# Loading batch 0's queries in halves, v of a pair in one load, and a lag for the Sinkhorn totals

## The chip, the cores and the metric

The kernel runs on one core of one Trainium2 chip. The metric is the device time of one execution in microseconds (us). The profiles list the program's instructions by engine: TensorE (PE, with its weight loads as PEld), VectorE (DVE), ScalarE (ACT), GpSimd (POOL, which here issues nearly all loads) and SyncE (SP). All runs compared here are fast; one run of the kernel before, at 988.76 us and a mean granted clock of 0.656, was slow and is left out.

## The reference, cut to what matters

Attention over 4 batches of 8 heads, 768 positions of 64 numbers, with a local band and 24 block summaries as keys. Its output is x (3072 x 512) for a mixture of 8 experts, all of which take every token, weighted by a matrix P that eight Sinkhorn rounds normalise by rows and columns. The attention lines are written shorter here than in the reference.

```python
k_sum = k.reshape(B, H, nb, 32, D).max(axis=3)
v_sum = v.reshape(B, H, nb, 32, D).mean(axis=3)
scores_l = scale * q @ k.T            # kept where |i - j| < 16
scores_s = scale * q @ k_sum.T + log(32)
out = softmax([scores_l, scores_s]) @ [v, v_sum]
...
P = np.exp(logits)
for _ in range(8):
    P /= P.sum(1, keepdims=True) + 1e-09
    P /= P.sum(0, keepdims=True) + 1e-09
    P *= N / E
for e in range(E):
    out += P[:, e:e+1] * (np.maximum(x @ w1[e], 0) @ w2[e])
```

## The kernel before

Heads are worked on in pairs, four pairs per batch. A small list scheduler (`Plan`) decides in Python, from estimated durations, in what order each engine gets its instructions. In the finished program that order is fixed, and in the runs below an engine whose next instruction is not ready waits for it: TensorE stands 3.0 us before two products whose data come late (no_lag), and only 1.7 us when the same products stand later in its order (the changed kernel).

The front, which the change is about, in cuts:

```python
def load_qk(i, z):                       # k or q of a pair, batch 0: one load
    ...
    nc.gpsimd.dma_start(
        out=t[:].rearrange("p j g d -> p j (g d)"),
        in_=src[b, h0:h0 + 2].rearrange("j (p g) d -> p j (g d)", g=G))

def load_v(i):                           # v of a pair: one load per head
    b, h0 = i // PB, (i % PB) * 2
    for j in range(2):
        nc.gpsimd.dma_start(out=v_x[i % NQ][:, :, j, 0:D],
                            in_=v[b, h0 + j].rearrange("(g p) d -> p g d", p=128))
...
nc.vector.memset(zeros, 0.0)
keep_busy(14)                            # 14 products of zeros
...
load_pair(0)                             # k, q, v
U["ident"] = last[0] = add("POOL", 0.35, ident_constant, [last[0]])
load_pair(1, "kq")
U["band"] = last[0] = add("POOL", 0.7, band_constants, [last[0]])
load_pair(2, "kq")
load_pair(1, "v")
load_pair(3, "kq")
load_pair(2, "v")
load_pair(3, "v")
for i in range(2):
    load(("w1", i), lambda i=i: load_w1_0(i), 0.85, 2.5)
load("w2", lambda: load_w2(0), 0.85, 5.0)
...
for i in range(PB):
    pair_start(i, i)                     # transposes of k and q, block maxima and sums
    pair_half(i, 0, i)                   # first halves of the queries
add("DVE", 1.6, late_constants, [U["mk", 0, 0]], 5.5)   # memsets that batch 1 needs
expert0(0, [U["x", i, 0] for i in range(PB)])           # expert 0 on the first halves
for i in range(PB):
    pair_half(i, 1, 10 + i)
...
plan.idle = (0.43, lambda: keep_busy(2), U["rl", 0, 0]) # fillers where PE would idle
```

And one round of Sinkhorn, in the "bridge" between attention and the seven remaining experts:

```python
for eng, us, fn, o, w in (("DVE", 0.5, rows, (), ()), ("POOL", 0.7, by_rows, (), ()),
                          ("DVE", 0.35, columns, (), ()), ("PE", 0.12, totals, [buf], ()),
                          ("DVE", 0.2, inverse, (), [buf]), ("POOL", 0.7, by_columns, (), ())):
    step = add(eng, us, fn, [step], -50.0, opens=o, uses=w)
```

The softmax here doesn't subtract the row's maximum and nothing guards it: scores larger than these inputs give would overflow.

## Time and profile before

The time was 687.12 us, the median of three runs. I cut the profiled execution into five parts.

| part | from, to | length in us |
|---|---|---|
| start | span start, first transpose of k | 5.71 |
| front | ... first product of expert 0's hidden layer | 21.12 |
| bulk | ... logits of the last batch | 101.65 |
| bridge | ... first product of the experts' second layer | 46.83 |
| tail | ... end | 509.79 |

### The profile page before, as it was taken

How to read it: one execution, taken by the hardware profiler on the slowest of the kernel's cores; microseconds unless marked ns; L12 is line 12 of the kernel's file. 1: busy time of each engine (PE TensorE's matmuls, PEld its weight loads, DVE VectorE, ACT ScalarE, POOL GpSimd, SP SyncE). 2: the span in 40 equal slices, each digit the busy share in tenths (PEclk: the TensorE clock that was granted, in tenths of full speed). 3: DMA queues.
4: the chain of work that ended last, by engine and by line, in shares of the span. 5: the costliest groups of instructions: out<-in, count | busy, mean ns of one | idle time of the engine just before them, and what ended most of it. 6: DMA issues, size and time to landing. Idle time of an engine off the chain costs nothing.

```text
span 685.1 us, 13613 instructions
## 1 busy us (share of the span) xinstructions
PE 673.9 (98%) x5195; PEld 439.0 (64%) x5195; DVE 590.4 (86%) x1440; ACT 404.7 (59%) x781; POOL 141.5 (21%) x189
## 2 busy tenths in 40 slices
PE   8999999999999999999999999999999999999996
PEld 4666656555666666666666666666666666666665
DVE  6779888797699998999889988998899888998886
ACT  5677677555677765555555555555555555555551
POOL 8599840121203120100101010201010101100000
PEclk9999999999999999999999999999999999999999
DMA  9999990000324023220513050403131051301224
GB/s 134 182 131 127 117 139 10 2 1 0 54 25 44 6 27 52 26 22 1 78 16 32 1 77 1 47 1 57 22 31 17 5 74 16 33 1 47 84 87 154
DMA packets 112786, 33.90 MB, mean 49 GB/s; under 512 B 98129, under 2 KB 109905, under 8 KB 112721
## 3 DMA queue, kind: packets, MB, share of 16 engines
q0 software_dynamic: 103840, 26.22, 40.3%
q1 hardware_dynamic: 8352, 6.80, 3.3%
q8 instruction: 41, 0.67, 0.4%
q14 instruction: 25, 0.20, 0.1%
q10 hardware_dynamic: 528, 0.02, 0.0%
HBM read 52.45 MB, written 6.29 MB: 86 GB/s over the span
## 4 chain that ended last, share of the span: by engine, by line
PE 85%; DVE 10%; issue 2%; DMA 1%; POOL 1%; ACT 0%; DVEq 0%; ACTq 0%
PE xy L837 32%; PE pg L831 14%; PE pb L831 9%; PE pa L831 9%; PE yps L204 6%; PE hps L199 6%; DVE hf L781 3%; DVE out_acc L974 2%; PE sg L301 1%; PE tkq L282 1%; DVE hf L892 1%; PE vs L309 1%; DVE hf L778 1%; DMA vx<-in_v_dram 1%; PE av L446 1%
## 5 line engine op out<-in xcount | busy, mean ns | idle before, releaser
L837 PEld LDWEIGHTS <-hf 128*128 128x128 f16 x2352 | 229.8, 98 | 99.2 <-issue 5.2
L837 PE MATMUL xy<-w,hf 128*128 128x256 f16 x1312 | 183.4, 273 | 0.0
L837 PE MATMUL xy<-ws,hf 128*128 128x256 f16 x984 | 147.6, 272 | 1.4
L190 ACT ACTIVATE hf<-pg 128x512 f16<-128x512 f32 x84 | 50.2, 597 | 158.2 <-PE pg L831 158.2
L974 DVE SCALAR_TENSOR_TENSOR out_acc<-xy,P_sb,out_acc 128x512 f32<-128x512 f32 x164 | 115.1, 744 | 1.7 <-PE xy L837 1.7
L778 DVE TENSOR_TENSOR hf<-hf 128x512 f16<-128x512 f16 x252 | 99.5, 422 | 3.2
L831 PE MATMUL pa<-xT,w 128*128 128x512 f16 x336 | 99.9, 379 | 0.0
L781 DVE TENSOR_TENSOR hf<-pb,c 128x512 f16<-128x512 f32 x84 | 58.0, 690 | 36.3 <-ACT xy L956 31.4
L831 PEld LDWEIGHTS <-w 128*128 128x128 f16 x672 | 65.6, 98 | 28.2 <-issue 0.5
L175 POOL DMA_DIRECT2D w<-in_moe_w_dram x56 | 41.8, 758 | 186.8 <-PE pg L831 181.3
L831 PEld LDWEIGHTS <-ws 128*128 128x128 f16 x504 | 49.3, 98 | 42.3 <-issue 0.2
L190 ACT ACTIVATE hf<-pa 128x512 f16<-128x512 f32 x84 | 50.2, 597 | 19.3 <-PE pa L831 19.3
L781 DVE TENSOR_TENSOR hf<-pg,c 128x512 f16<-128x512 f32 x84 | 57.2, 681 | 0.3
L850 ACT COPY pg<-pa 128x512 f32<-128x512 f32 x84 | 47.9, 570 | 5.0 <-PE pa L831 0.3
L831 PE MATMUL pg<-xTs,w 128*128 128x512 f16 x168 | 50.0, 379 | 0.1
L831 PE MATMUL pb<-xT,ws 128*128 128x512 f16 x168 | 50.0, 379 | 0.0
L831 PE MATMUL pb<-xTs,ws 128*128 128x512 f16 x168 | 50.0, 379 | 0.0
L831 PE MATMUL pg<-xTs,ws 128*128 128x512 f16 x168 | 50.0, 379 | 0.0
L858 ACT COPY c<-pb 128x512 f32<-128x512 f32 x84 | 49.7, 592 | 0.4 <-ACT pg L850 0.4
L831 PE MATMUL pg<-xT,w 128*128 128x512 f16 x168 | 49.8, 377 | 0.0
L199 PE MATMUL hps<-xT,w 128*128 128x384 f16 x256 | 49.3, 326 | 0.0
L865 ACT COPY c<-pg 128x512 f32<-128x512 f32 x84 | 48.7, 579 | 0.3 <-PE pg L831 0.3
(135 smaller groups left out, 859.6 us busy)
## 6 DMA issues: line engine op xcount, KB each, us to landing
w<-in_moe_w_dram POOLq DMA_DIRECT2D x8, 1024.0 KB, 9.2
w<-in_moe_w_dram POOLq DMA_DIRECT2D x56, 128.0 KB, 3.5
out_dram<-out_acc SPq DMA_DIRECT2D x22, 256.0 KB, 2.1
vx<-in_v_dram POOLq DMA_DIRECT2D x32, 96.0 KB, 4.9
kst<-in_k_dram POOLq DMA_DIRECT2D x24, 96.0 KB, 4.5
qst<-in_q_dram POOLq DMA_DIRECT2D x24, 96.0 KB, 4.3
w<-in_moe_w_dram POOLq DMA_DIRECT2D x2, 512.0 KB, 7.8
kst<-in_k_dram POOLq DMA_DIRECT2D x4, 192.0 KB, 4.9
```

The lines of the kernel that those rows point to most:

```text
L175: nc.gpsimd.dma_start(out=t[:, :, h, :], in_=moe_w1[e].rearrange("(dk p) f -> p dk f", p=128)[:, :, f:f + 128])
L190: nc.scalar.activation(out=out, in_=in_, func=AF.Relu, bias=0.0, scale=1.0)
L199: nc.tensor.matmul(hp[:, 0:n], lhsT=w1s[e][:, dk, 128 * f:128 * (f + 1)], rhs=xT[:, dk, t0:t0 + n], start=(dk == 0), stop=(dk == KD - 1))
L204: nc.tensor.matmul(yp[:], lhsT=h[:, f, c * 128:(c + 1) * 128], rhs=w2s[e][:, f, :], start=(f == 0), stop=(f == KF - 1))
L778: nc.vector.tensor_tensor(out=out, in0=in0, in1=in1, op=ALU.subtract)
L781: nc.vector.tensor_tensor(out=out, in0=in0, in1=in1, op=ALU.add)
L831: nc.tensor.matmul(bank[:], lhsT=w[:, dk, :], rhs=x[:, dk, :], start=start and dk == 0, stop=dk == KH - 1, skip_group_check=True)
L837: nc.tensor.matmul(bank, lhsT=a(f)[:, 128 * c:128 * (c + 1)], rhs=w[:, f, :], start=start and f == 0, stop=f == FH - 1, skip_group_check=True)
L850: nc.scalar.copy(out=B["g"][:], in_=B["a"][:])
L858: nc.scalar.copy(out=B["c5"][:], in_=B["b"][:])
L865: nc.scalar.copy(out=B["c2"][:], in_=B["g"][:])
L974: nc.vector.scalar_tensor_tensor(out=acc, in0=src, scalar=P_sb[:, t, e:e + 1], in1=acc, op0=ALU.mult, op1=ALU.add)
```

## The change

It wants the data of batch 0 earlier. The second halves of its queries are used only after the first halves of all four pairs, so they are loaded later, behind the first half of w1. The tile of v gets its heads outermost, so that one load serves a pair. v comes ahead of the next pair's k. Apart from that, the product that totals the Sinkhorn columns is given a lag in the plan, so that PE's order puts it later. The core of the diff (the changed indices of `sv`, seven lines, and the split transposes and copies are cut; so are two estimates of the plan, which hold for all batches: 0.95 in place of 1.65 us for a load of v, and 0.4 us for the transposes of k or q of a pair, where it had 0.53 in batch 0 and 0.34 later):

```diff
-        v_x = [attn.tile([128, G, 2, VD], BF16, name=f"vx{i}") for i in range(NQ)]
+        v_x = [attn.tile([128, 2, G, VD], BF16, name=f"vx{i}") for i in range(NQ)]
...
-            for j in range(2):
-                nc.gpsimd.dma_start(out=v_x[i % NQ][:, :, j, 0:D],
-                                    in_=v[b, h0 + j].rearrange("(g p) d -> p g d", p=128))
+            nc.gpsimd.dma_start(out=v_x[i % NQ][:, :, :, 0:D].rearrange("p j g d -> p (j g) d"),
+                                in_=v[b, h0:h0 + 2].rearrange("j (g p) d -> p (j g) d", p=128))
+
+        def load_qh(i, h):
...
+            nc.gpsimd.dma_start(
+                out=at["st", i, 1][:, h].rearrange("p j g d -> p j (g d)"),
+                in_=q[0, 2 * i:2 * i + 2, h * HS:(h + 1) * HS].rearrange("j (p g) d -> p j (g d)", g=HG))
...
+                nc.vector.memset(t[:, W + HS:W + HS + W], 0.0)
...
-        load_pair(0)
+        load_pair(0, "k0v")
         U["ident"] = last[0] = add("POOL", 0.35, ident_constant, [last[0]])
-        load_pair(1, "kq")
+        load_pair(1, "k0")
         U["band"] = last[0] = add("POOL", 0.7, band_constants, [last[0]])
-        load_pair(2, "kq")
         load_pair(1, "v")
-        load_pair(3, "kq")
-        load_pair(2, "v")
-        load_pair(3, "v")
-        for i in range(2):
-            load(("w1", i), lambda i=i: load_w1_0(i), 0.85, 2.5)
+        load_pair(2, "k0v")
+        load_pair(3, "k0v")
+        zero_w1(0)
+        for i in range(PB):
+            load_pair(i, "1")
+        zero_w1(1)
         load("w2", lambda: load_w2(0), 0.85, 5.0)
...
-                    step = add(eng, us, fn, [step], -50.0, opens=o, uses=w)
+                    step = add(eng, us, fn, [step], -50.0, opens=o, uses=w, lag=(0.9 if n else 2.0) if fn is columns else 0.0)
```

More of the change, by code (lines that the diff above doesn't have):

```diff
@@ L267, in load_v, with tr_qh, tr_qh_out @@
             b, h0 = i // PB, (i % PB) * 2
-            for j in range(2):
-                nc.gpsimd.dma_start(out=v_x[i % NQ][:, :, j, 0:D],
-                                    in_=v[b, h0 + j].rearrange("(g p) d -> p g d", p=128))
+            nc.gpsimd.dma_start(out=v_x[i % NQ][:, :, :, 0:D].rearrange("p j g d -> p (j g) d"),
+                                in_=v[b, h0:h0 + 2].rearrange("j (g p) d -> p (j g) d", p=128))
+        def load_qh(i, h):
+            if h == 0:
+                at["st", i, 1] = attn.tile([128, 2, 2, HG, D], BF16, tag="qst", name="qst", bufs=NQ)
+            nc.gpsimd.dma_start(
+                out=at["st", i, 1][:, h].rearrange("p j g d -> p j (g d)"),
+                in_=q[0, 2 * i:2 * i + 2, h * HS:(h + 1) * HS].rearrange("j (p g) d -> p j (g d)", g=HG))
+        def tr_qh(i, h):
+            st, t = at["st", i, 1], bank("m", "tkq", BF16)
+            at["t", i, 1] = t
+            for g in range(HG):
+                for j in range(2):
+                    nc.tensor.transpose(t[64 * j:64 * j + 64, g * 128:(g + 1) * 128], st[:, h, j, g, :], ident)
+        def tr_qh_out(eng, i, h):
+            copy(eng, qT[i][:, W + h * HS:W + (h + 1) * HS].rearrange("c (p g) -> c p g", g=HG),
+                 at.pop(("t", i, 1))[:, 0:HS].rearrange("c (g p) -> c p g", g=HG))
         def tr(i, z, tag):
@@ L309, in block_sums @@
                 nc.tensor.matmul(vs.rearrange("p (j d) -> p j d", j=2), lhsT=m_blk[:, g, :],
-                                 rhs=sv[:, g, :, 0:D], start=(g == 0), stop=(g == G - 1))
+                                 rhs=sv[:, :, g, 0:D], start=(g == 0), stop=(g == G - 1))
         def block_out(i):
@@ L329, in near_values @@
                 nc.sync.dma_start(out=ve[q0 + W:q0 + 2 * W, 1:G, c0:c0 + VD],
-                                  in_=sv[128 - W:128, 0:G - 1, j, :])
+                                  in_=sv[128 - W:128, j, 0:G - 1, :])
                 nc.sync.dma_start(out=ve[q0:q0 + W, 0:G - 1, c0:c0 + VD],
-                                  in_=sv[0:W, 1:G, j, :])
+                                  in_=sv[0:W, j, 1:G, :])
         def scores(i, h):
@@ L373, in values @@
                     nc.tensor.matmul(av[:, o + j * VD:o + (j + 1) * VD],
-                                     lhsT=em[:, j, c, :], rhs=sv[:, c, j, :],
+                                     lhsT=em[:, j, c, :], rhs=sv[:, j, c, :],
                                      start=(cc == 0 and j == 0), stop=False,
@@ L450, in values_h @@
                 for j in range(2):
-                    mm(0, 128, cc, j, em[:, j, cc, 2 * W:2 * W + 128], sv[:, HG * h + cc, j, :],
+                    mm(0, 128, cc, j, em[:, j, cc, 2 * W:2 * W + 128], sv[:, j, HG * h + cc, :],
                        start=(cc == 0 and j == 0))
@@ L456, in values_h @@
                     if c + 1 < G:
-                        mm(96, 128, cc, j, em[0:32, j, cc + 1, 0:32], sv[0:32, c + 1, j, :])
+                        mm(96, 128, cc, j, em[0:32, j, cc + 1, 0:32], sv[0:32, j, c + 1, :])
                     if c > 0:
                         mm(0, 32, cc, j, em[96:128, j, cc - 1 if cc else HG, LIVE:PADL],
-                           sv[96:128, c - 1, j, :])
+                           sv[96:128, j, c - 1, :])
             for cc in range(HG):
@@ L589, in load_pair @@
                 if c == "v":
-                    load(("v", i), lambda: load_v(i), 1.65, 1.75,
+                    load(("v", i), lambda: load_v(i), 0.95, 1.75,
                          [U.get(("A", old, 1)), U.get(("near", old))])
+                elif c in "01":
+                    load(("q", i, int(c)), lambda c=int(c): load_qh(i, c), 0.75, 0.55)
                 else:
@@ L601, in pair_start @@
             tag = "m" if i < PB else "a"
-            for z in range(2):
+            for z in range(2 if i >= PB else 1):
                 buf = Buffer(tag)
-                U["tr", i, z] = add("PE", 0.53 if i < PB else 0.34, lambda z=z: tr(i, z, tag),
+                U["tr", i, z] = add("PE", 0.4, lambda z=z: tr(i, z, tag),
                                     [U["kq"[z], i], U["ident"]] + (war_k, war_q)[z]
@@ L610, in pair_start @@
                                     uses=[buf])
+            if i < PB:
+                query_half(i, 0, prio)
             U["km", i] = add("DVE", 0.95, lambda: key_max(i), [U["kT", i, 0]] + war_q[2:], prio)
@@ L616, in pair_start, with query_half @@
                              prio + 0.01, uses=[buf])
+        def query_half(i, h, prio):
+            buf = Buffer("m")
+            U["tr", i, 1] = add("PE", 0.25, lambda: tr_qh(i, h),
+                                [U["q", i, h], U["ident"], U["tr", i, 0] if h == 0 else U["kT", i, 1]], prio,
+                                opens=[buf])
+            U["kT", i, 1] = add({"ACT": 0.46, "DVE": 0.5}, 0, lambda: tr_qh_out(U["qT", i, h].on, i, h),
+                                [U["tr", i, 1]], prio, uses=[buf])
+            U["qT", i, h] = U["kT", i, 1]
         def pair_half(i, h, prio):
+            if h:
+                query_half(i, 1, prio)
             n = PB * h + i
@@ L714, with zero_w1 @@
         last[0] = add("POOL", 1.3, None)
-        load_pair(0)
+        def zero_w1(i):
+            load(("w1", i), lambda: load_w1_0(i), 0.85, 2.5)
+        load_pair(0, "k0v")
         U["ident"] = last[0] = add("POOL", 0.35, ident_constant, [last[0]])
-        load_pair(1, "kq")
+        load_pair(1, "k0")
         U["band"] = last[0] = add("POOL", 0.7, band_constants, [last[0]])
-        load_pair(2, "kq")
         load_pair(1, "v")
-        load_pair(3, "kq")
-        load_pair(2, "v")
-        load_pair(3, "v")
-        for i in range(2):
-            load(("w1", i), lambda i=i: load_w1_0(i), 0.85, 2.5)
+        load_pair(2, "k0v")
[4 more added lines that the diff above has]
+        zero_w1(1)
         load("w2", lambda: load_w2(0), 0.85, 5.0)
```

## The prediction

> **What bounds the kernel now.** I read the page first, then the chain of waits in order of time, the timeline of the front, the stretches (busy time per window), and the waits of the tensor engine. The page says that PE is the bound almost everywhere.
>
> ```profile
> PE 673.9 (98%) x5195; PEld 439.0 (64%) x5195; DVE 590.4 (86%) x1440; ACT 404.7 (59%) x781; POOL 141.5 (21%) x189
> ...
> PE 85%; DVE 10%; issue 2%; DMA 1%; POOL 1%; ACT 0%; DVEq 0%; ACTq 0%
> ```
>
> So only time in which PE idles, turns over filler, or runs at a lower clock can be won. A busy PE may be doing filler: line 522 multiplies zeros [...]while the first pairs of heads are on their way. The stretches, first for all instructions and then for tile "idle" alone (the filler), show where.
>
> ```profile
> 0.00:5.70 5.70, 4.64 (x14) 1.65 (x14) 3.21 (x51) 1.49 (x2) 4.43 (x11) 1.00 0.67 78
> 5.70:14.40 8.70, 7.45 (x119) 4.27 (x120) 5.19 (x17) 5.46 (x7) 8.47 (x13) 1.00 1.54 161
> 14.40:17.84 3.44, 3.23 (x29) 1.65 (x30) 3.08 (x7) 1.66 (x3) 3.14 (x5) 0.50 2.07 167
> 17.84:26.82 8.98, 8.85 (x148) 5.65 (x142) 6.66 (x20) 5.70 (x9) 5.59 (x7) 1.00 1.27 204
> 26.82:40.00 13.18, 13.18 (x176) 8.62 (x173) 9.74 (x24) 9.81 (x18) 9.46 (x12) 1.00 2.07 146
> ```
> ```profile
> 5.70:14.40 8.70, 2.93 (x11) 1.00 1.54 161
> 14.40:17.84 3.44, 1.03 (x2) 0.50 2.07 167
> 17.84:26.82 8.98, 1.64 (x6) 1.00 1.27 204
> 26.82:40.00 13.18, 0.00 (x0) 1.00 2.07 146
> ```
>
> Columns: length, then busy time of PE, weight load, DVE, ACT and POOL with counts, then granted clock, DMA share, GB/s. From 26.82 us on, when expert 0's hidden layer can start (it needs the first halves of all four pairs of batch 0), PE is full of real work. Before it, 19 filler products run, PE stands still for 1.25 us in the first of these windows, and the clock is half for 3.44 us. POOL, which issues the loads, is busy 8.47 of 8.70 us. Why it is so late, the chain tells:
>
> ```profile
> 8.47 0.83 POOL vx L269
> 9.29 6.48 DMA vx<-in_v_dram
> 15.81 0.85 PE vs L309 x6
> 16.66 0.97 PE idle L522 x2
> ```
>
> Pair 1's v, issued behind k and q of pairs 1 and 2, lands only at 15.8 us, and the chain goes through it. After 27 us the one other place with PE gaps is the Sinkhorn stage (129 to 163 us):
>
> ```profile
> PE sink L1033 <- DVE csum_sb L1028: 1.2, 3, 0.8
> ...
> PEld sink L1033 <- DVE csum_sb L1028: 2.3, 4, 0.7
> ```
>
> [...]the stretch at 0.50 lasts 3.44 us, and PE's gaps of 0.52 and 0.73 us lie just ahead of it (12.82 and 14.08 us in the timeline). [...]161 GB/s while k, q and v (768-byte and 128-byte packets) move, 204 GB/s while w1 and w2 (1024 bytes) do. [...]The issue of k or q for two heads takes 0.72 us, that of v of one head, with three times the pieces, only 0.85, so v of two heads in one issue should cost about 1.0 and not 1.7 us.
>
> **The change, part by part.**
>
> (1) v in one issue. It takes 2 x 0.85 - 1.0 = 0.7 us off POOL per pair (an estimate from those rows). The bytes and their 128-byte packets stay, and value products and block sums are as many and as wide as before. In batches 1 to 3 POOL is the pace of the loads (POOL busy 50.7 of the 55 us from 40 to 95), so they finish perhaps 8 us earlier, but PE is busy 54.8 of those 55 us anyway: worth nothing there.
>
> (2) Queries in halves. Before the last v of batch 0, 12 loads of 192 KB (2.36 MB) go out; at 161 GB/s that is 14.7 us, from 3.0 to 17.7. Now a pair needs k, half of q and v: 0.49 MB, four pairs 1.97 MB, 12.2 us. Between the first v and k of pair 1, POOL still waits for the identity, whose memset comes after DVE's constants (4.5 us), so I allow 0.6 us of empty queue. The last v then lands near 15.8, some 1.9 us earlier. What counts more: v of pair 1 comes third in line and not fourth, at about 11 instead of 15.8 us.
>
> PE does the same 12 query transposes per pair, six early and six late; copies go from one of 0.80 us to two of some 0.46 (an estimate, from the 0.48 of the 384-wide copy of xT). The added memset (0.07 us on DVE, four times) comes before the data.
>
> When does the hidden layer start? k of pair 3 lands near 14 to 14.5 us. Its way on, by durations of this trace: transposes 0.53, kT copy 0.80, qT copy 0.46, scores 0.39, exponential 1.00, masks 0.81, values 0.86, normalisation 0.76, transposes 0.34, copy 0.48: 6.4 us, [...]8.2 us. That gives 22.2 to 22.7, and 23 with a little queueing, against 26.8.
>
> That is not a gain of 3.8 us, as less real work lies before it. From the pieces of the chain, a first half costs PE 0.46 + 0.46 (transposes) + 0.34 (scores) + 0.27 (summaries) + 0.47 (block sums) + 0.86 (values) + 0.27 (xT) = 3.13 us, four 12.5. Before 26.8 us scores and summaries of two second halves also ran (2 x 0.61). So 21.1 us (5.7 to 26.8) held 13.7 us of work: 7.4 us lost. It checks: 17 fillers at 0.22 and two at 0.43 are 4.6, gaps 1.6, and real work in the slow window lost 1.1. After the change the 17.3 us to 23.0 hold 12.5 - 4 x 0.23 = 11.6 us: 5.7 us lost. Gain 1.7 us, or 2.2 if query transposes of the second halves get in before 23.
>
> (3) Order of the weights. The first half of w1 (0.52 MB at 204 GB/s) follows v of pair 3 and lands near 19, the late query halves near 21.5, the second half of w1 near 24, w2 near 29 as before, since the bytes up to it are the same. From 23 to 29 PE has 5.2 us of hidden layer and two of the second halves: enough.
>
> (4) The lag after the column sums. It only moves PE's "totals" product later in PE's order, 2.0 us in the first round and 0.9 in the others, behind other products instead of ahead of them. Of the 1.2 us of PE gaps I credit 0.7. The rounds get longer, by at most some 5 us; the last write of P_sb, at 163 us, becomes about 167, before the first use (after 175 us, where the bridge ends): hidden.
>
> The sum: 1.9 + 0.7 = 2.6 us off 687.1, so 684.5.
>
> **The rivals.** (a) ACT takes the place of the loads. It has 0.80 + 0.46 + 1.00 + 0.47 + 0.48 = 3.2 us per first half, as long as the 3.05 us that the DMA now takes per pair. From 6.3 us four pairs end at 19.1 at best, plus the last pair's path past its exponential, 22.5. For it: balance so close that both wait on each other; it limits the gain to about 2.2 us in the front, and with queueing gives 685. (b) The clock falls to half again[...]. A window of 3.4 us at half clock costs up to 1.7 us if it falls on real work: 686. Against it: the waits on v that made the gap go away. (c) The saved loads are only put off: the late query halves and w2 are waited for after 23 us. For it: the total bytes until w2 are unchanged; against it: the reserve of work counted in (3). It would give 686 to 687. (d) The front works better than I count, without filler gaps and with early second halves: up to 4.5 us of the 7.4 lost, 682. A loss beyond the old time would need the Sinkhorn chain to run past 175 us; nothing in the profile suggests it.
>
> **Range and chances.** The central sum is 2.6 us. Rival (d) with the whole Sinkhorn gap gives 5.5 less, so 681.6; (b) and (c) give 686 to 687. The three runs of before differ by 1.3 us. I take 682.2 to 686.6. A change of 2% would be 13.7 us, more than all idle time and filler of the front and Sinkhorn together, so within 2% is all but sure.
>
> **What would show it.** v of pair 1 ends its wait near 11 us and not 15.8. The first hidden product (line of hidden_mm) starts near 23 us; filler after 5.7 us is less than 19 products; no, or a shorter, half clock window; POOL's issues of v take about 1.0 us each, and the loads of the last pair are issued some 8 us earlier; the sink product's waits fall from 1.2 us to below 0.5; from 175 us to the end the same length, 510 us. The prediction is wrong if the first hidden product starts after 25 us, if PE then waits for w2 or late queries, or if the part after 175 us changes length.

Passages that no trace or run of this case shows are cut out of the recorded text, and the cuts are marked. No term of the sum is among them: it stays 1.9 us for the front and 0.7 us for Sinkhorn, 2.6 us off 687.1, so 684.5. In the way on from k of pair 3, the 8.2 us are the 6.4 us of the durations listed and 1.8 us allowed for hand-overs, an estimate. In the trace of before, steps on pair 3's way begin 0.03 to 0.23 us after the step ahead of them: the exponential 0.05 us after the scores (21.73 to 21.78 us), the masks 0.23 us after the exponential (22.78 to 23.01).

## More of the kernel before

The stretches of the kernel before with the cuts there. The columns are length; busy time of PE, PEld, DVE, ACT and POOL, each with its number of instructions; mean granted clock; DMA share; GB/s.

```profile
5.71:26.83 21.12, 19.53 (x288) 11.58 (x287) 14.94 (x42) 12.83 (x19) 17.19 (x23) 0.92 1.51 180
26.83:128.48 101.65, 101.45 (x1168) 63.31 (x1165) 83.53 (x218) 74.03 (x119) 60.16 (x74) 1.00 1.36 100
128.48:175.31 46.83, 45.64 (x261) 23.37 (x259) 35.69 (x94) 25.54 (x50) 9.79 (x16) 1.00 0.00 1
175.31:685.10 509.79, 502.67 (x3473) 339.08 (x3471) 453.06 (x1036) 290.78 (x593) 49.87 (x66) 1.00 0.25 38
```

PE is idle for 1.59 us in the front and 1.19 us in the bridge, and for next to nothing in the bulk. The clock of 0.92 in the front is one stretch of 3.41 us at half clock.

## The result, and the profile after

685.78 us (median of four runs, 685.37 to 686.57) against 686.74 us (four runs, 685.85 to 687.16). The ratio is 0.9989 with a 95% interval of 0.9972 to 1.0006: no change that is clear of noise. Ratios here are the mean time of one kernel's fast runs over that of the other's of the same rounds, so not quite the ratio of the medians.

The page of the changed kernel, in the two lines that the prediction showed of before:

```profile
PE 671.8 (98%) x5191; PEld 438.7 (64%) x5191; DVE 590.8 (86%) x1445; ACT 406.8 (59%) x784; POOL 134.6 (20%) x177
...
PE 85%; DVE 12%; issue 2%; ACT 1%; DVEq 0%; ACTq 0%
```

DMA and POOL have gone from the chain that ended last, and DVE has grown from 10% to 12%. The five parts of the changed kernel (all but the start), to be read against the table above:

```profile
6.79:26.08 19.29, 17.48 (x284) 10.86 (x283) 15.61 (x44) 12.55 (x21) 16.44 (x21) 1.00 1.46 168
26.08:127.08 101.00, 100.60 (x1164) 62.72 (x1161) 82.67 (x218) 75.89 (x119) 53.26 (x63) 1.00 1.44 105
127.08:174.21 47.13, 45.42 (x265) 24.04 (x263) 35.96 (x94) 26.04 (x51) 10.05 (x16) 1.00 0.01 1
174.21:684.00 509.79, 502.54 (x3473) 339.13 (x3471) 453.25 (x1036) 290.80 (x593) 50.03 (x66) 1.00 0.25 38
```

So, in the profiled pair: start +1.08, front -1.83, bulk -0.65, bridge +0.30, tail 0.00, together -1.10 us, from a span of 685.1 to one of 684.0. The front gave what was promised and no clock was lost in it. But the start lost 1 us, and the bridge, for which 0.7 us were promised, got longer.

Where the start and the front of the changed kernel spend their time is told by its chain of waits (start, length, what):

```profile
1.07 5.79 PE idle L539 x14
6.86 0.47 PE tkq L296 x12
...
10.63 0.38 DVE Ee L588
...
13.02 0.17 DVE col_en L593
...
13.22 0.21 DVE rc L493
...
13.45 0.57 DVE xs L494
...
14.06 0.36 PE tx L501 x3
```

Two things to see. First, the 14 products of zeros now hold the first transpose until 6.86 us, though the kernel has as many as before: the clock rose at 6.37 us in this execution and at 4.19 us in the profiled one of before, and until it rises the fillers start 0.43 us apart in place of 0.22. Second, no load is on the chain any more. In its place stand the late constants, 2.6 us of DVE memsets (10.63 to 13.19 us), behind which the normalisation of pair 0 waits.

### The profile page after: what moved, and what is told of

Read it like the earlier page. It is cut to its first block, busy times and chain, and to the rows that moved or that the text cites. A ratio compares the mean times of both kernels' runs of the same rounds, so it can differ in the third digit from the quotient of the medians.

```text
span 684.0 us, 13584 instructions
## 1 busy us (share of the span) xinstructions
PE 671.8 (98%) x5191; PEld 438.7 (64%) x5191; DVE 590.8 (86%) x1445; ACT 406.8 (59%) x784; POOL 134.6 (20%) x177
## 4 chain that ended last, share of the span: by engine, by line
PE 85%; DVE 12%; issue 2%; ACT 1%; DVEq 0%; ACTq 0%
PE xy L873 32%; PE pg L867 14%; PE pb L867 10%; PE pa L867 9%; PE yps L204 6%; PE hps L199 6%; DVE hf L817 3%; DVE out_acc L1010 2%; PE sg L318 1%; DVE hf L928 1%; PE tkq L299 1%; PE idle L539 1%; DVE hf L814 1%; PE tx L501 1%; PE av L463 1%
```

## The experiments

Twelve kernels were run, each with one profile and five rounds of timing. This table gathers the parts of each profile. "Half" is the time at half clock ahead of the first hidden product, or reaching into it. Each ratio is against runs of the kernel before in the same rounds; medians of different rows can come from different rounds.

| kernel | clock rise | first transpose | front | half | bulk | bridge | median | ratio to before, 95% interval |
|---|---|---|---|---|---|---|---|---|
| before | 4.19 | 5.71 | 21.12 | 3.4 | 101.65 | 46.83 | 686.74 | 1 |
| changed | 6.37 | 6.79 | 19.29 | 0 | 101.00 | 47.13 | 685.78 | 0.9989 (0.9972 to 1.0006) |
| lag_only | 5.84 | 6.53 | 22.30 | 6.8 | 101.65 | 44.97 | 685.99 | 0.9988 (0.9970 to 1.0006) |
| no_lag | 3.76 | 5.50 | 19.51 | 0 | 101.24 | 49.23 | 688.18 | 1.0027 (1.0013 to 1.0041) |
| late_after | 7.00 | 7.10 | 18.70 | 0 | 99.30 | 48.18 | 687.24 | 1.0005 (0.9990 to 1.0020) |
| late_before | 4.40 | 5.82 | 22.99 | 3.4 | 101.99 | 46.83 | 688.95 | 1.0031 (1.0018 to 1.0043) |
| late2_after | 5.03 | 6.12 | 18.52 | 0 | 99.76 | 48.18 | 684.55 | 0.9963 (0.9948 to 0.9978) |
| late2_before | 4.72 | 5.97 | 21.39 | 0 | 100.70 | 48.23 | 687.83 | 1.0006 (0.9992 to 1.0021) |
| lag_more | 5.40 | 6.30 | 22.65 | 6.8 | 101.01 | 47.01 | 687.28 | 0.9996 (0.9975 to 1.0016) |
| filler9_after | 4.39 | 5.08 | 20.13 | 0 | 101.01 | 47.13 | 685.65 | 0.9984 (0.9967 to 1.0001) |
| order_only | 6.19 | 6.70 | 21.79 | 0 | 100.83 | 49.29 | 690.17 | 1.0045 (1.0029 to 1.0061) |
| halves_2v | 4.79 | 6.01 | 22.95 | 10.2 | 99.27 | 48.25 | 688.75 | 1.0022 (1.0004 to 1.0039) |
| filler9_before | 6.47 | 5.04 | 23.69 | 6.8 | 101.65 | 46.83 | 686.27 | 1.0000 (0.9983 to 1.0018) |
| combo3 | 5.11 | 5.08 | 19.99 | 0 | 99.76 | 48.18 | 684.80 | 0.9973 (0.9957 to 0.9989) |

The tail is 509.71 to 510.32 us in all fourteen, so nearly everything is decided ahead of it.

### 1 and 2: the lag alone, and the change without it

```diff
 # lag_only: the kernel before, with
-step = add(eng, us, fn, [step], -50.0, opens=o, uses=w)
+step = add(eng, us, fn, [step], -50.0, opens=o, uses=w, lag=(0.9 if n else 2.0) if fn is columns else 0.0)
 # no_lag: the changed kernel, with the same line turned back
```

> The kernel before with the Sinkhorn lag alone. Theory A (the prediction's): the lag takes 0.7 us of PE waits away, time 0.7 us below before. Theory B (read off the changed kernel's trace, where the first sink product still waits 0.78 us and the second 0.93): the waits only move from round to round, time within 0.3 us of before and the sink waits of PE still 1.0 us or more.

> The changed kernel without the lag. Theory A: 0.7 us slower than the changed kernel (near 686.5). Theory B: the same as the changed kernel within 0.3 us (685.5 to 686.1).

By its time alone, lag_only fits theory A (0.12% are 0.8 us), with an interval that includes 1. The stage itself says that both theories are too small. The lag is worth much more than either had it: the bridge goes from 46.83 to 44.97 us on the old front (-1.86), and from 49.23 to 47.13 on the new one (-2.10). And without the lag the change is a loss, 1.0027 times the time of before, with an interval that excludes 1. So what gain there is comes with the lag alone, too (medians of 685.99 us, and 685.78 with both parts of the change: the same within the noise), and the new loads alone lose. The stretch of the bridge in lag_only and in no_lag, then the waits of PE for the column sums in no_lag and in the changed kernel (total, times, longest):

```profile
130.48:175.45 44.97, 44.41 (x261) 23.85 (x259) 34.88 (x92) 26.36 (x52) 9.58 (x16) 1.00 0.00 1
```
```profile
126.25:175.48 49.23, 46.16 (x265) 23.75 (x263) 35.98 (x94) 26.13 (x51) 9.17 (x16) 1.00 0.00 1
```
```profile
PE sink L1069 <- DVE csum_sb L1064: 3.0, 2, 1.6
```
```profile
PE sink L1069 <- DVE csum_sb L1064: 1.7, 2, 0.9
```

In the kernel before the same wait was 1.2 us, and in lag_only no such line is left. So the new front makes the Sinkhorn stage 2.40 us longer (46.83 to 49.23), of which 3.0 - 1.2 = 1.8 us stand in these waits. That is as much as the front itself gained. A front that is planned otherwise leaves PE and DVE in other positions of the plan when Sinkhorn begins, and PE reaches its totals before DVE has the sums. That the plan's estimates are the root of it is an argument from the code; that the waits appear with the new front and shrink with the lag is measured. With the lag, too, the new front costs the bridge 2.16 us (44.97 to 47.13). The two changed estimates for later batches could have a part in this; that they are not needed for it is shown by order_only (experiment 10), which leaves them as they were and gets the same waits.

### 3 and 4: the late constants, moved a little

```diff
 # late_after: the changed kernel; late_before: the kernel before
-add("DVE", 1.6, late_constants, [U["mk", 0, 0]], 5.5)
+add("DVE", 1.6, late_constants, [U["mk", PB - 1, 0]], 5.5)
```

> The changed kernel with the late constants (2.6 us of DVE memsets, needed by batch 1 only) moved from behind the first mask of pair 0 to behind that of pair 3. Theory C: with the loads earlier, these memsets are the new wait of the front (they lie on the chain from 10.6 to 13.2 us); the first hidden product starts 1.5 to 2.5 us earlier against the first transpose and the time falls by 1.0 to 2.0 us, to about 684.3. Rival D: ACT and the hand-overs hold the front just as much; the time stays within 0.4 us of the changed kernel's.

> The kernel before with the same move of the late constants. Theory C: there the load of v of pair 1 (landing at 15.8 us) held the front, and the memsets ended at 13.2 us, well before it; moving them gains 0.4 us at most. Rival D': the memsets held the front in the kernel before too; then the move gains 1 us or more here as well, and the loads were never the bound.

A miss, and a useful one. late_after's front is 18.70 us, 0.6 shorter than the changed kernel's, and its time is no better; late_before is slower by 0.31%, which neither theory had. The DVE timeline of late_after shows what I had done (start, length, instruction):

```profile
20.50 0.66 DVE L447 TENSOR_TENSOR Eh<-erh,band 128x960 bf16<-128x960 bf16 x1
21.07 0.15 DVE L452 TENSOR_TENSOR Eh<-erh,band 32x32 bf16<-32x32 bf16 x1
21.36 0.79 DVE L588 MEMSET Ee<- 64x384 uint32 x2
...
23.76 0.17 DVE L593 MEMSET col_en<- 128x128 f32 x1
23.96 0.20 DVE L493 RECIPROCAL rc<-av 128x6 f32<-128x6 f32 x1
```

The memsets now stand between the masks and the normalisation of pair 3, on the very path to the first hidden product. And DVE works without a gap from 11.7 to 24.7 us: shifting the block inside the full engine won nothing here.

### 5 and 6: the late constants out of the front

```diff
 # late2_after: the changed kernel; late2_before: the kernel before
-add("DVE", 1.6, late_constants, [U["mk", 0, 0]], 5.5)
...
 for i in range(PB):
     pair_half(i, 1, 10 + i)
+U["late"] = add("DVE", 2.6, late_constants, [U["mk", 0, 1]], 5.5)
 # and U["late"] among the dependencies of batch 1's near values, block sums and edges
```

> The changed kernel with the 2.6 us of late memsets moved out of the front altogether (behind the first mask of the second halves). Theory E: after the change the front (first transpose to first hidden product, 19.3 us) is bound by DVE, which in the earlier attempt ran without a gap from 11.7 to 24.7 us with the memsets merely shifted inside it; the front shrinks by 1.5 to 2.6 us, to 17 to 17.8 us. Rival D (ACT and hand-overs bind): the front stays above 18.7 us. What of it reaches the end is open, since the Sinkhorn stage can take it back (between none and 2 us).

> The kernel before with the same move. If v of pair 1 (landing at 15.8 us) bound its front, as the prediction read, the front (21.1 us with one half-clock window, about 20 without) shrinks by less than 1 us. If DVE bound it there too, it shrinks by 2 us or more.

late2_after is the fastest of all: 0.9963, interval 0.9948 to 0.9978, so it beats the kernel before clear of noise. Its median is 1.2 us below the changed kernel's, measured in other rounds; the two intervals touch, so that it beats the changed kernel too is likely and not shown. Theory E is right about the direction only: the front is 18.52 us where 17 to 17.8 was expected. The waits of PE say why:

```profile
PE vs L326 <- DMA vx<-in_v_dram: 1.0, 2, 0.7
```

With DVE's 2.6 us gone, PE stands before the block sums and waits for v again, a wait that the changed kernel did not have. So after the change loads and DVE bound the front about equally, and each hides what is taken from the other. On the old front the same move wins nothing (21.39 us, ratio 1.0006), which fits that the load of v was the longer wait there: PE waits 1.5 us for it.

### 7: more lag

```diff
 # lag_more: the changed kernel, with
-lag=(0.9 if n else 2.0) if fn is columns else 0.0
+lag=((3.5, 2.0)[n] if n < 2 else 0.9) if fn is columns else 0.0
```

> The changed kernel with the lag of the first two Sinkhorn rounds raised from 2.0 and 0.9 to 3.5 and 2.0 us. Theory F: the bridge (last logits to first product of the second layer, 47.1 us) still holds 1.7 us of PE waits for the column sums of the first two rounds because the planned order is early there; they go and the bridge falls to about 45.5 us, the time by 1 to 1.5 us. Rival G: PE is short of other ready work there (DVE's sums of xT and w1 bind), so other waits take their place and the bridge stays within 0.4 us.

Rival G holds. The waits for the column sums are gone but for 0.2 us, and others have come: of PE for DVE's sums of x and for its relu.

```profile
PE pg L867 <- DVE xT L814: 0.8, 1, 0.8
...
PE yps L204 <- DVE h L192: 0.5, 1, 0.5
```

The bridge is 47.01 us, 0.12 less than with the smaller lag. This run showed something else, by accident. Its order of PE instructions is the same as the changed kernel's up to the Sinkhorn stage. Yet here is its front, which in the changed kernel took 19.29 us at a clock of 1.00:

```profile
6.30:28.95 22.65, 20.19 (x283) 12.42 (x282) 15.79 (x43) 12.67 (x21) 17.74 (x24) 0.85 1.46 172
```

The same program, 3.36 us longer, with 6.8 us at half clock.

### 8 and 9: fewer fillers at the start

```diff
 # filler9_after: the changed kernel; filler9_before: the kernel before
-keep_busy(14)
+keep_busy(9)
```

> The changed kernel with 9 instead of 14 products of zeros at the start. Theory H: the moment at which the clock rises (3.8 to 7.1 us in six profiles) depends on the execution and not on the kernel, and where it is late, 14 fillers at half clock hold the first transposes until 7 us; with 9 they start before 6 us in any case. The time falls by 0 to 1.2 us and its spread shrinks. Rival I: with less filler the clock rises later or falls again, so real work runs at half clock: the first hidden product is no earlier and the time equal or up to 1.5 us longer.

> The kernel before with 9 instead of 14 products of zeros at the start, to compare with the changed kernel treated the same way, free of the luck of when the clock rises. Theory J: at equal start the changed kernel is 1 to 2 us faster (its front is shorter by 0.8 to 1.8 us, its bulk by 0.6, its bridge longer by 0.3); so this one lands at 686.5 to 687.5. Rival K: the gain of the changed kernel was clock luck; both land within 0.5 us (685.2 to 686.2).

The clock rose anywhere between 3.76 and 7.00 us in the fourteen profiles, though the first filler starts at 1.05 or 1.06 us in every one. The three profiles with 9 fillers (4.39, 5.11 and 6.47 us) lie inside the range of those with 14, so a later rise, as in rival I, is not shown; half clock after the rise came in filler9_before (6.8 us) and not in filler9_after. With 14 fillers the first transpose came at 5.50 to 7.10 us, with 9 at 5.04 to 5.08 us, so the first half of theory H holds. The second does not: filler9_after has 685.65 us against 685.78, and no smaller spread. Its front is 20.13 us, 0.84 longer than the changed kernel's: PE, early, waits 1.5 us for v. Between theories J and K the pair decides little. The medians differ by 0.62 us, which lies between the two forecasts; the ratios differ by 0.16% (1.1 us), at the low end of theory J's, and the two intervals overlap.

### 10: the order of the loads alone

```diff
 # order_only: the kernel before, with
-        load_pair(2, "kq")
         load_pair(1, "v")
-        load_pair(3, "kq")
-        load_pair(2, "v")
-        load_pair(3, "v")
+        load_pair(2)
+        load_pair(3)
```

> The kernel before with nothing but the order of its loads changed: whole queries, v still in two loads per pair, but v of pairs 1 and 2 ahead of the next pair's k and q. The prediction's claim that v of pair 1 coming earlier counts most: the wait of the block sums for v of pair 1 ends near 12 instead of 15.8 us, and the front is 0.5 to 1 us shorter at the same number of half-clock windows. Rival: the DMA engines are busy without a break, so k and q of pairs 2 and 3 come later by as much as v comes earlier; the front is unchanged within 0.4 us. Time within 0.7 us of before in both cases.

Slower, by 0.29 to 0.61%, which neither side expected. v of pair 1 lands at 12.38 us, where it was 15.77, and is no longer waited for. But the front is 21.79 us without any half clock, so longer than it would be in the kernel before, and k and q of pairs 2 and 3 come later (k of pair 3 at 18.04 us, where it was 16.33); 26 fillers run after the first transpose, eight more. And the bridge is 49.29 us, with 3.1 us of waits for the column sums, as in no_lag. So v ahead of k does not pay by itself; with the smaller q and the single load of v, the same order gives fronts of 19.29 (changed) and 19.51 us (no_lag), also without half clock. Which of the two makes the difference was not tested apart.

### 11: v in two loads again

```diff
 # halves_2v: the changed kernel, with
-            nc.gpsimd.dma_start(out=v_x[i % NQ][:, :, :, 0:D].rearrange("p j g d -> p (j g) d"),
-                                in_=v[b, h0:h0 + 2].rearrange("j (g p) d -> p (j g) d", p=128))
+            for j in range(2):
+                nc.gpsimd.dma_start(out=v_x[i % NQ][:, j, :, 0:D],
+                                    in_=v[b, h0 + j].rearrange("(g p) d -> p g d", p=128))
 # and 1.65 instead of 0.95 us for it in the plan
```

> The changed kernel with v of a pair in two loads again (layout kept, heads outermost). If the single issue matters only to POOL (prediction: worth nothing while PE is full), the time stays within 0.5 us of the changed kernel's and the front within 0.5 us; POOL's issues of v cost 1.7 us per pair and the last load of batch 3 goes out some 8 us later. Rival: POOL's issue rate holds the front of the changed kernel; then the front grows by 0.7 us or more per pair in which v is waited for (1 to 2 us).

The front of the profile is 22.95 us, 3.7 longer, and the median 688.75 us. That looks like the rival, but the runs one by one tell a finer story. Those of halves_2v and lag_only, with the mean granted clock of each:

```
halves_2v   685.88 (0.999)  688.04 (0.991)  688.63 (0.991)  688.87 (0.991)  688.96 (0.991)  689.07 (0.991)
lag_only    683.80 (0.998)  684.89 (0.999)  685.00 (0.999)  686.98 (0.995)  687.12 (0.995)  687.15 (0.995)
```

At a clock of 0.999 the time is 685.88 us, that of the changed kernel. In the five other runs the clock was 0.991, and the profile, taken of one of them, shows 10.2 us at half clock from 15.03 us on. The landings agree: k of pair 3 lands at 16.90 us with two loads and at 16.91 with one, v of pair 3 at 19.27 and 18.89. So the 0.7 us of POOL's time brought the loads forward by little, and what this front lost, it lost to the clock. Five of six runs lost clock here and 5 of 16 with the new front (counted below), but that the single load helps to keep the clock was not shown.

### 12: both edits that seemed to help

combo3 is late2_after with 9 fillers in place of 14.

> The changed kernel with both edits that helped: late memsets out of the front, and 9 fillers at the start. If they add up: 683.5 to 684.3, first transposes before 5.5 us. If the earlier start only turns into waits for the loads (as with 9 fillers alone, where the block sums waited 1.5 us for v): 684.3 to 685.

684.80 us, ratio 0.9973: they do not add up. The first transpose comes 1.0 us earlier than in late2_after and the first hidden product 0.4 us later; PE waits 1.3 us for v and 0.8 us for k.

### When the clock fell in the profiles

All fourteen profiles have the time at which the clock rises, and in the six in which it falls again in the front, it falls and comes back a multiple of 3.413 us after the rise (in the kernel before it rises at 4.19, falls at 14.43 and is back at 17.84 us, 3 and 4 times 3.413 us later; the changed kernel has one fall, at 682.21 us, 198 times 3.413 us after its rise at 6.37). So I laid a grid of 3.413 us from the rise in all fourteen (for those without a fall in the front that is an assumption), and read PE's busy time in each window of it ahead of the first hidden product (transposes and fillers count as busy). Here are the windows before a fall in the kernel before and in halves_2v, and the emptiest one of the changed kernel:

```profile
11.02:14.43 3.41, 2.16 (x39) 1.17 (x33) 2.73 (x11) 1.77 (x3) 3.26 (x5) 1.00 1.69 172
```
```profile
11.62:15.03 3.41, 1.97 (x31) 1.22 (x31) 2.94 (x12) 1.38 (x3) 3.41 (x6) 1.00 1.64 143
```
```profile
13.20:16.60 3.40, 2.27 (x40) 1.48 (x41) 3.27 (x9) 2.11 (x4) 3.05 (x5) 1.00 1.68 149
```

The clock fell after six windows, in which PE was busy for 1.92 to 2.16 of 3.41 us. It held after all others: one of 2.12 us (order_only), and otherwise 2.23 us or more. No single gap of PE in the window before the fall was above 1.35 us in halves_2v. That is what these fourteen profiles show; a rule for other kernels was not tested. The return of the clock did not follow this share: in lag_only PE was busy for all 3.41 us of the first window at half clock and the clock stayed at half, in the kernel before it was busy for 3.20 us and the clock rose. The changed kernel's emptiest window holds 0.11 us more than the fullest one before a fall (2.27 us against 2.16), and its clock held; in lag_more, the same program up to there with its grid placed otherwise, it holds 1.92 us, and the clock fell. late2_after's emptiest window holds 2.62 us, for PE waits there 0.4 us at a time for a normalisation, where the changed kernel waits 1.0 us at 13 to 14 us for that of pair 0; none of its six runs has a mean clock below 0.998. Against the kernel before that may be part of why it is the fastest. Against the changed kernel it can't be, since that kept its clock in all four runs (0.999 in each); there the two profiles differ by -0.67 us in the start, -0.77 in the front, -1.24 in the bulk, +1.05 in the bridge and +0.3 in the tail.

For a run without a profile, its mean clock has to do: in the fourteen profiles it is 0.998 or 0.999 without a window at half clock in the front, 0.996 or 0.997 with one, 0.993 to 0.995 with two and 0.991 with three. Counted by these numbers, an estimate, the front of before (the kernel before in the later rounds, and lag_only) lost clock in 10 of 38 fast runs. The new front (changed, no_lag and lag_more, whose orders of PE instructions are the same up to the Sinkhorn stage) lost it in 5 of 16: none of the 4 of the changed kernel, 1 of 6, 4 of 6. So the new front does not hold the clock better, and the changed kernel's four clean runs are luck.

Runs at 0.998 or more can be compared without the clock:

| kernel | runs | lowest to highest | median |
|---|---|---|---|
| before | 25 | 685.83 to 687.34 | 686.64 |
| lag_only | 3 | 683.80 to 685.00 | 684.89 |
| no_lag | 5 | 687.53 to 688.82 | 688.10 |
| changed | 4 | 685.37 to 686.57 | 685.78 |

These are few runs, of different rounds, so the table is a hint. It says that the lag alone is worth 1.8 us, and that the new loads cost 0.9 us with the lag and 1.5 us without. The sums of bulk and bridge point the same way: 148.48 us before, 146.62 lag_only, 150.47 no_lag, 148.13 changed.

## Why the prediction was right or wrong

The time, 685.78 us, lies within 682.2 to 686.6, and "within 2%" was right. The gain was 1.0 us between the medians, and 1.10 in the profiled pair, where 2.6 had been forecast; and it came about otherwise than said. That the time fell inside the range is in part luck: the changed kernel's four runs kept their clock, and the range reached up to the rivals' 686.

**The front, 1.9 us forecast, 1.83 measured: right in sum by luck, wrong in cause.** The kernel did lose four fillers (14 after the first transpose, where it had 18; the prediction's 19 counts the tail of the fourteenth of the start, too), and the block sums of pair 1 ran at 12.55 us without a wait. But real work before the first hidden product did not shrink to 11.6 us: all four late query transposes and the scores and summaries of two second halves fitted in before it, as the "2.2 us" variant had it and more. And 1.1 us of the old 7.4 us lost, as I had computed myself, was the half-clock window, which the changed kernel's profile did not have. Where both fronts ran with two such windows they took 22.30 us (lag_only) and 22.65 us (lag_more): no gain. "What counts more: v of pair 1 comes third in line" failed as a cause (it had been fifth after pair 0's v, not fourth): order_only brought that v forward by 3.4 us, and was slower. Of the rivals, (a) had the right shape, but what took the loads' place was not ACT but DVE, with 2.6 us of memsets that I had seen in the trace and left out of the sum.

**The start was not in the sum at all.** I took 5.7 us as given. With the same 14 fillers the first transpose came at 5.50 us where the clock rose at 3.76 (no_lag), and at 7.10 us where it rose at 7.00 (late_after). That is luck, and cost the changed kernel's profile 1.08 us.

**The first hidden product at 23 us was wrong**: 26.08 us in the profile, so my own condition for failure ("after 25 us") was met. The term that failed is "k of pair 3 lands near 14 to 14.5 us". In the trace of the changed kernel (issued at 10.5 us, 6.4 us to landing) it lands at 16.91 us, and in the kernel before at 16.33: the change did not bring it forward. With v of pair 2 now ahead of it, it was issued at 10.50 us, where it had been 10.10. The way on was well estimated: 8.2 us forecast, 8.1 (late2_after), 8.8 (no_lag) and 9.2 us (changed) measured, the last two with the memsets in it. By that path 16.91 us gives 25.1 us at best. (The chain of the changed kernel does not name this load, as its transposes begin 1.0 us after the landing, at 17.95 us; DVE's memsets are what the chain shows.) The estimate had loads run back to back from 3.0 us at 161 GB/s; by this the last v of the kernel before landed at 17.7 us, but its trace has 20.29, so the misfit could be seen beforehand. The last v came forward by 1.4 us (from 20.29 to 18.89), where 1.9 was forecast. No run moved k of pair 3 alone, so that it holds the first hidden product is read from the traces and not shown by experiment.

**The Sinkhorn stage, 0.7 us forecast, failed twice.** The lag was mis-sized: 1.9 to 2.1 us, against a credit of 0.7 out of 1.2 us of visible waits. And a term was missing: the new front costs the bridge 2.4 us. Together the bridge got 0.30 us longer, and the sink waits rose from 1.2 to 1.7 us where "below 0.5" was forecast. That the longer rounds are hidden was right: the tail did not move.

**Rival (b), the clock, was named and underrated.** "Against it: the waits on v that made the gap go away": the gap stayed, behind DVE's memsets (0.98 us in the changed kernel, where it had been 0.73), and with the same front the clock held in the changed kernel's profile, where the emptiest window of the grid had PE busy for 2.27 us, and fell in lag_more's, where it had 1.92 us.

**POOL's part was right but for one size**: an issue of v for a pair takes 1.02 to 1.17 us in the changed kernel (median 1.04; one for a single head took 0.84 us in the kernel before), and the last v of batch 3 goes out at 80.5 instead of 85.2 us, 4.7 us earlier and not 8, and worth nothing there.

Two slips of the sum changed nothing: rival (d) with the whole Sinkhorn gap is 4.5 + 1.2 = 5.7 us and not 5.5, and the half-clock stretch is 3.41 us, not 3.44.

Open: why the bulk is 0.65 us shorter, and what makes the clock rise again. The changed kernel itself has four timed runs, so its gain of about 1 us stays inside the noise.

## What to carry to other kernels

When instruction order is fixed from estimates, a gain at one end can turn into waits at the other (in no_lag the front is 1.61 us shorter than before, and the waits for the column sums are 3.0 us against 1.2): look at every later stage where engines meet, and undo the parts of a change singly, since here the change without one of its parts lost 0.27%, and that part alone did as well as the whole. An estimate of when a load lands should first be tried on the kernel before, whose trace has the answer. Note for each profile when the clock rose and fell before comparing two of them: the same program took 19.3 us for its front at full clock and 22.7 us with 6.8 us at half clock. An engine that is full has to be relieved of work: with the memsets moved within DVE, which then had no gap from 11.7 to 24.7 us, the time was no better (late_after, 687.24 us against 685.78 of the changed kernel), and with them out of the front it was 684.55 us (late2_after).
